# A layer norm, attention and GEGLU block on one core: one PSUM copy of the gate with the gelu on GpSimd, down tiles in pairs at a lag of five, and P times V every second step

## The chip, the cores and the metric

The kernel runs on one core of one Trainium2 chip. A core has TensorE (PE, matmuls into PSUM), VectorE (DVE), ScalarE (ACT), GpSimd (POOL) and SyncE (SP), whose queue issues nearly all DMAs here. Each engine works through its own queue in order; a wait for another engine holds everything behind it. The metric is the device time of one execution in microseconds (us), lower is better.

## The reference

```python
def _A_ref(x, wqkv, wo):                      # 32 heads of 18
    qkv = (x @ wqkv).reshape(B, S, 3, H, Dh)...
    scores = einsum("bhqd,bhkd->bhqk", q, k) * (Dh ** -0.5)
    p = softmax(scores)
    return einsum("bhqk,bhkd->bhqd", p, v)... @ wo

def _B_ref(x, w_gate, w_up, w_down):
    g = x @ w_gate
    u = x @ w_up
    return (gelu(g, approximate=True) * u) @ w_down

xn = layernorm(x)                             # (1, 2048, 576)
out = x + _A_ref(xn, ...) * silu(_B_ref(xn, ...))
```

S is 2048, the model width D 576, the hidden width F 4608. All is float32. The gelu is the tanh form: 0.5 g (1 + tanh(0.798 (g + 0.0447 g^3))).

## The kernel before

Float32 products are made from float16 pieces: the normed input is kept transposed as a high and a low part (XHT, XL), weights are split into whi and wlo, and three matmuls (high by high, high by low, low by high) are accumulated in PSUM. P times V alone runs in float32.

**Attention is the outer loop.** Heads are taken two at a time, 16 pairs, each in 32 steps (s): 2 halves of the queries (qh) by 16 blocks of 128 keys (kt). In a step qk2 makes two score tiles of 128 keys by 512 queries for two heads (L935, two matmuls of 64 rows side by side), and an exp on ScalarE writes them as P (L941). Beside each, qk1 (L895) makes a score tile of the next pair, of which DVE takes the row maxima (L898, into PM); both score tiles have one PSUM buffer each. pv (L957) multiplies P and V of the step before, four matmuls in four column strips. After step 29 max_end reduces the maxima of the next pair (L907 to L910), transposes them on PE (L916) and writes them through DRAM (md, L920) into two rows of the next pair's QT (L922). norm divides by the softmax sums, through small DMAs.

**Everything else is filler.** A generator yields the other matmuls one by one: the V and Q, K projections, then 18 chunks (c) of 256 hidden columns, each for four blocks (sb) of 512 tokens. For a chunk and block, gu makes two gate tiles g and two up tiles u (ft 0 and 1; 14 matmuls of 512 columns each, L289 to L294), and dn four down tiles of 128 tokens in two halves of 288 columns (six matmuls each, L485), which DVE accumulates into Y (L496). fill(amt) issues filler until the planned PE time amt is used up; a step calls it four times.

**Deferred work.** What follows a tile on DVE, ScalarE or GpSimd isn't issued where the tile ends but at a later tick: subtick() ahead of each fill advances a counter, issues what is due, and one piece of the next chunk's weight preparation (prep: maxima, splits L231 and L234). defer.at(now + n, f) puts f at the n-th tick from now. As each engine's queue is in order, the tick decides behind which exp or which row maximum such work stands.

**The m banks.** Gate, up and down tiles, the transpose of L916 and the projections share three PSUM banks, m, in rotation: a tile's first matmul waits until the readers of the tile three before it are done (MTile, with the number of readers).

The gelu of before reads g from PSUM three times: a square on ScalarE (L425), a product on DVE (L429), tanh on ScalarE (L434), a product with g again on DVE (L437), then with u (L450); ScalarE writes the high half of h (L459) and GpSimd the low half (L463). dn of the block before runs behind each up tile, four m tiles in a row.

Of the kernel before, what the change touches and what calls it, by code (L numbers as in the profile page):

```python
# [20 lines left out]
P = 128  # L21
NT = S // P
# [45 lines left out]
def kernel(ctx: ExitStack, tc: tile.TileContext, x, wqkv, wo, w_gate, w_up, w_down, out):  # L68
# [55 lines left out]
    def prep(name, parts, n, down=None, urgent=False, lead=0):  # L124
# [74 lines left out]
        def scales():  # L199
# [120 lines left out]
    def proj_j_sb(w, j, part, sb, mt=None, wait=0):  # L320
# [7 lines left out]
        def hi():  # L328
            ev["h"] = wp.tile([P, 512], F16, tag="evh", name=f"evh_{j}_{part}_{sb}")
            nc.scalar.activation(ev["h"][0:n], mt.t[0:n], AF.Copy, scale=2.0 ** -22)  # L330
            mt.done()

        def lo():
            ev["l"] = wp.tile([P, 512], F16, tag="evl", name=f"evl_{j}_{part}_{sb}")
# [82 lines left out]
    def gu(w, c, sb, ft):  # L417
        s0 = 512 * sb
        g = MTile([P, 512], F32, 3)
        yield from mm_wx(g.t, w, 0, P * ft, P * ft + P, s0, s0 + 512)  # L420
        st = {}

        def sq():
            st["z"] = wp.tile([P, 512], F32, tag="sz", name=f"sz_{c}_{sb}_{ft}")
            nc.scalar.activation(st["z"], g.t, AF.Square, scale=w.uE[:, 0:1])  # L425
            g.done()

        def zz():
            nc.vector.scalar_tensor_tensor(st["z"], st["z"], 1.0 / GC, g.t, op0=ALU.add, op1=ALU.mult)  # L429
            g.done()  # L430

        def th():
            st["t"] = wp.tile([P, 512], F32, tag="tw", name=f"tw_{c}_{sb}_{ft}")
            nc.scalar.activation(st["t"], st["z"], AF.Tanh, scale=w.uE[:, 1:2])  # L434

        def ww():
            nc.vector.scalar_tensor_tensor(st["t"], st["t"], 1.0, g.t, op0=ALU.add, op1=ALU.mult)  # L437
            g.done()
# [8 lines left out]
        yield from mm_wx(u.t, w, 1, P * ft, P * ft + P, s0, s0 + 512)  # L447

        def hp():
            nc.vector.scalar_tensor_tensor(st["t"], st["t"], 2.0 ** -54, u.t, op0=ALU.mult, op1=ALU.mult)  # L450
            u.done()

        def hhi():
# [5 lines left out]
            nc.scalar.activation(hstate[c, sb].hi[:, ft], st["t"], AF.Copy)  # L459

        def hlo():
            hs = hstate[c, sb]
            nc.gpsimd.tensor_tensor(hs.lo[:, ft], st["t"], hs.hi[:, ft], op=ALU.subtract)  # L463
# [9 lines left out]
    def dn(w, c, sb, tiles):  # L473
        until(lambda: (c, sb) in hstate and hstate[c, sb].n == 2)
        hs = hstate[c, sb]
        for si in tiles:
# [658 lines left out]
```

## Time and profile before

| | |
|---|---|
| median of three runs (lowest, highest) | 3055.71 us (3055.68, 3059.48) |
| the profiled execution | 3058.35 us, of which its span is 3056.6 us |
| granted TensorE clock, mean | 0.977 |
| PE busy in 1000 to 1200 us / ScalarE / DVE / GpSimd | 192.6 / 114.8 / 152.9 / 12.8 us of 200 |
| from the start to the first exp of attention | about 188 us |
| from pair to pair of heads, pairs 1 to 15 | 174.9 us |

How to read the rows of the prediction: a row of the timeline has start and length in us, then engine, line, operation, output <- inputs, shapes, and in brackets how long the engine stood idle before and what ended that. A row of waits has the engine and line that waited, what it waited for, the sum in us, how often, and the longest. A row of groups has count, then busy us and the mean ns of one, then the idle time before and its releasers. PE's records overlap, since matmuls are pipelined: starts are compared, not lengths.

### The profile page before, as it was taken

The page shows a single profiled execution, that of the slowest core. Times are in us where ns is not written, and L with a number is a line of the kernel's source. Part 1 is how long each engine was busy: PE and PEld are TensorE (multiplying, and loading weights), DVE is VectorE, ACT ScalarE, POOL GpSimd, SP SyncE. Part 2 cuts the span into 40 slices and gives each one's busy share as a digit, 9 for nine tenths or more (in the row PEclk, how much of TensorE's full clock was granted, in tenths as well). Part 3 has the DMA queues.
Part 4 walks back from the last instruction along what each step waited for, and adds up shares of the span by engine and source line. Part 5 has one row for each costly group of instructions (what it writes and reads, how often), then busy time and mean ns, then how long its engine had stood idle before and what let it go on. Part 6 is the DMA issues. An engine that isn't in the chain of part 4 may idle for free.

```text
span 3056.6 us, 43746 instructions
## 1 busy us (share of the span) xinstructions
PE 2817.5 (92%) x17732; PEld 1051.1 (34%) x17732; DVE 2229.5 (73%) x3055; ACT 1614.9 (53%) x1948; POOL 203.4 (7%) x220
## 2 busy tenths in 40 slices
PE   5899889999999999999999999999999999999877
PEld 5443223333333333333333333333333333333334
DVE  6766567777677877777786877777777868777594
ACT  4135455555565555555555555565555555565531
POOL 3000000000000000000000000000000000000000
PEclk9899999999999999999999999999999999999988
DMA  3233311010011011010101011001111010101113
GB/s 119 80 85 81 92 37 45 13 44 12 28 23 31 20 36 45 13 31 20 31 21 35 20 36 44 13 11 40 31 20 36 20 36 23 31 5 33 29 48 116
DMA packets 135872, 117.39 MB, mean 38 GB/s; under 512 B 59957, under 2 KB 113973, under 8 KB 135669
## 3 DMA queue, kind: packets, MB, share of 16 engines
q1 hardware_dynamic: 135092, 113.42, 13.5%
q8 instruction: 138, 2.26, 0.3%
q10 hardware_dynamic: 576, 1.18, 0.1%
q14 instruction: 66, 0.53, 0.1%
HBM read 84.95 MB, written 29.61 MB: 37 GB/s over the span
## 4 chain that ended last, share of the span: by engine, by line
PE 73%; DVE 18%; DMA 4%; issue 2%; ACT 2%; SPq 1%; POOL 0%; ACTq 0%; DVEq 0%; POOLq 0%
PE m L289 26%; PE pv L957 14%; PE m L485 10%; PE s L935 9%; DVE PM L898 8%; PE s L895 7%; PE m L302 2%; PE m L292 2%; PE m L294 2%; DVE sg L542 1%; DMA KD<-evh 1%; DVE tw L450 1%; DVE y L496 1%; DVE tw L437 1%; DVE m_c L163 1%
## 5 line engine op out<-in xcount | busy, mean ns | idle before, releaser
L898 DVE TENSOR_REDUCE PM<-s 128x2 f32<-128x1024 f32 x1024 | 1251.6, 1224 | 632.2 <-PE s L895 623.6
L941 ACT ACTIVATE P<-s,etab 128x1024 f32<-128x1024 f32 x896 | 997.1, 1113 | 939.1 <-PE s L935 927.5
L957 PE MATMUL pv<-P,VT 128*32 128x512 f32 x4096 | 553.1, 612 | 2.1 <-DMA VT<-VS 2.1
L289 PE MATMUL m<-XHT,whi_c 128*128 128x512 f16 x1152 | 438.5, 381 | 20.7 <-DVE y L496 18.7
L289 PE MATMUL m<-XHT,wlo_c 128*128 128x512 f16 x1152 | 439.0, 381 | 0.0
L289 PE MATMUL m<-XL,whi_c 128*128 128x512 f16 x1152 | 438.7, 381 | 0.0
L935 PE MATMUL s<-QT,KT 56*128 56x512 f16 x2048 | 403.1, 390 | 33.7 <-ACT P L941 33.2
L895 PE MATMUL s<-KT,QT 54*128 54x512 f16 x2048 | 395.8, 382 | 28.8 <-DMA QT<-QD 18.1
L485 PE MATMUL m<-dhi_c,hhi 128*128 128x288 f16 x1152 | 332.5, 289 | 62.9 <-DVE tw L450 28.8
L289 PEld LDWEIGHTS <-whi_c 128*128 128x128 f16 x2304 | 211.6, 98 | 407.8 <-issue 236.2
L463 POOL TENSOR_TENSOR hlo<-tw,hhi 128x512 f16<-128x512 f32 x144 | 167.2, 1161 | 2557.2 <-ACT hhi L459 2367.0
L485 PE MATMUL m<-dhi_c,hlo 128*128 128x288 f16 x1152 | 332.7, 289 | 0.0
L485 PE MATMUL m<-dlo_c,hhi 128*128 128x288 f16 x1152 | 332.5, 289 | 0.0
L485 PEld LDWEIGHTS <-hhi 128*128 128x128 f16 x2304 | 216.4, 98 | 271.0 <-issue 205.9
L496 DVE SCALAR_TENSOR_TENSOR y<-m,c_c,y 128x288 f32<-128x288 f32 x544 | 262.7, 504 | 13.1 <-PE m L485 12.7
L935 PEld LDWEIGHTS <-KT 56*128 56x128 f16 x2048 | 99.6, 92 | 426.1 <-issue 425.9
L289 PEld LDWEIGHTS <-wlo_c 128*128 128x128 f16 x1152 | 112.5, 98 | 205.3 <-issue 111.5
L957 PEld LDWEIGHTS pv<-P,VT 128*32 128x32 f32 x4096 | 81.2, 108 | 212.5 <-issue 209.9
L943 ACT ACTIVATE P<-s,etab 128x512 f32<-128x512 f32 x128 | 87.9, 687 | 116.2 <-PE s L935 110.5
L485 PEld LDWEIGHTS <-hlo 128*128 128x128 f16 x1152 | 112.9, 98 | 88.1 <-issue 64.0
L434 ACT ACTIVATE tw<-sz,uE_c 128x512 f32<-128x512 f32 x144 | 103.3, 717 | 58.0 <-DVE sz L429 58.0
L459 ACT ACTIVATE hhi<-tw 128x512 f16<-128x512 f32 x144 | 90.0, 625 | 66.9 <-DVE tw L450 66.9
(163 smaller groups left out, 2464.3 us busy)
## 6 DMA issues: line engine op xcount, KB each, us to landing
draw_c<-in_B_w_down SPq DMA_DIRECT2D x18, 576.0 KB
raw_c<-in_B_w_gate SPq DMA_DIRECT2D x18, 512.0 KB
raw_c<-in_B_w_up SPq DMA_DIRECT2D x18, 512.0 KB
obr<-rd SPq DMA_DIRECT2D x30, 256.0 KB
KT<-KD SPq DMA_DIRECT2D x32, 224.0 KB
QT<-QD SPq DMA_DIRECT2D x32, 216.0 KB
VS<-vst SPq DMA_DIRECT2D x16, 304.0 KB
VT<-VS SPq DMA_DIRECT2D x16, 304.0 KB
```

What stands on the lines that cost most here:

```text
L289: nc.tensor.matmul(o, lw[:, t, i, c0:c1], xx[:, t, s0:s1], start=(k == 0), stop=False)
L434: nc.scalar.activation(st["t"], st["z"], AF.Tanh, scale=w.uE[:, 1:2])
L459: nc.scalar.activation(hstate[c, sb].hi[:, ft], st["t"], AF.Copy)
L463: nc.gpsimd.tensor_tensor(hs.lo[:, ft], st["t"], hs.hi[:, ft], op=ALU.subtract)
L485: nc.tensor.matmul(mt.t[:, 0:288], a[:, ft, sl], b[:, ft, ms], start=(k == 0), stop=(k == 5))
L496: nc.vector.scalar_tensor_tensor(yy, mt.t[:, 0:288], w.c, yy, op0=ALU.mult, op1=ALU.add)
L895: nc.tensor.matmul(s1[:, h], QT[p][r, P * qt:P * qt + P], KT[p][r, 512 * kb:512 * kb + 512], start=True, stop=True)
L898: nc.vector.tensor_reduce(PM[p][:, :, qt, kb:kb + 1], s1, op=ALU.max, axis=AX.X)
L935: nc.tensor.matmul(s2[:, h], KT[p][r, P * kt:P * kt + P], QT[p][r, 512 * qb:512 * qb + 512], start=True, stop=True)
L941: nc.scalar.activation(pt, s2, AF.Exp, scale=ETAB[j0])
L943: nc.scalar.activation(pt[:, 0], s2[:, 0], AF.Exp, scale=ETAB[j0])
L957: nc.tensor.matmul(o[qd:qd + 32, :], VT[p][:, c0:c0 + 32], pt[:, h], start=(kt == 0), stop=(kt == NT - 1), skip_group_check=True,)
```

## The change

1. The gate is read from PSUM once: ScalarE copies it, scaled, to SBUF (gs). The cubic (three operations), the added one and the product with the up tile's part run on GpSimd, tanh stays on ScalarE. DVE makes u times g from PSUM and the copy (gv). The gate's m tile has one reader instead of three. The ticks of the chain change with it.
2. Down tiles are queued (dnq). Behind each gate tile and behind each up tile one 128-token unit (two m tiles) is taken, if more than five units are queued.
3. P times V is issued in every even step for the two steps before; the two fills behind it get nothing, and the other six of two steps each a third of a step's share instead of a quarter. P has six buffers instead of four.
4. max_end's transpose comes at the third tick instead of the second. The evacuation tiles evh and evl of the projections have three buffers instead of two.

```diff
@@ def prep
-                nc.vector.tensor_scalar(
-                    w.uE[:, 1:2], w.E[:, 0:1], GK * GC * 2.0 ** -24, None, op0=ALU.mult
-                )
+                nc.vector.tensor_scalar(w.uE[:, 1:2], w.s[:, 0:1], 2.0 ** -44, None, op0=ALU.mult)
@@ def proj_j_sb
-            ev["h"] = wp.tile([P, 512], F16, tag="evh", name=f"evh_{j}_{part}_{sb}")
+            ev["h"] = wp.tile([P, 512], F16, tag="evh", name=f"evh_{j}_{part}_{sb}", bufs=3)
...
@@ def gu
-        g = MTile([P, 512], F32, 3)
+        st = {}
+        gp = nc.gpsimd
+        g = MTile([P, 512], F32, 1)
         yield from mm_wx(g.t, w, 0, P * ft, P * ft + P, s0, s0 + 512)
-        def sq():
-            nc.scalar.activation(st["z"], g.t, AF.Square, scale=w.uE[:, 0:1])
-        def zz():
-            nc.vector.scalar_tensor_tensor(st["z"], st["z"], 1.0 / GC, g.t, op0=ALU.add, op1=ALU.mult)
-        def th():
-            nc.scalar.activation(st["t"], st["z"], AF.Tanh, scale=w.uE[:, 1:2])
-        def ww():
-            nc.vector.scalar_tensor_tensor(st["t"], st["t"], 1.0, g.t, op0=ALU.add, op1=ALU.mult)
+        def copy():
+            nc.scalar.activation(st["g"], g.t, AF.Copy, scale=w.uE[:, 0:1])
+            g.done()
+        def cubic():
+            gp.tensor_tensor(st["t"], st["g"], st["g"], op=ALU.mult)
+            gp.tensor_scalar(st["t"], st["t"], GC, 1.0, op0=ALU.mult, op1=ALU.add)
+            gp.tensor_tensor(st["t"], st["t"], st["g"], op=ALU.mult)
+        def th():
+            nc.scalar.activation(st["t"], st["t"], AF.Tanh, scale=GK)
+        def one():
+            gp.tensor_scalar(st["t"], st["t"], 1.0, 1.0, op0=ALU.mult, op1=ALU.add)
         t0 = defer.now
-        defer.at(t0 + 1, sq)
-        defer.at(t0 + 2, zz)
-        defer.at(t0 + 3, th)
-        defer.at(t0 + 4, ww)
+        defer.at(t0 + 1, copy)
+        defer.at(t0 + 2, cubic)
+        defer.at(t0 + 5, th)
+        defer.at(t0 + 6, one)
+        yield from dn_unit()
         u = MTile([P, 512], F32, 1)
         yield from mm_wx(u.t, w, 1, P * ft, P * ft + P, s0, s0 + 512)
+        def mul():
+            nc.vector.scalar_tensor_tensor(
+                st["v"], u.t, w.uE[:, 1:2], st["g"], op0=ALU.mult, op1=ALU.mult
+            )
+            u.done()
         def hp():
-            nc.vector.scalar_tensor_tensor(st["t"], st["t"], 2.0 ** -54, u.t, op0=ALU.mult, op1=ALU.mult)
-            u.done()
+            gp.tensor_tensor(st["v"], st["v"], st["t"], op=ALU.mult)
...
-        t1 = max(defer.now, t0 + 4)
-        defer.at(t1 + 1, hp)
-        defer.at(t1 + 2, hhi)
-        defer.at(t1 + 3, hlo)
+        t1 = defer.now
+        t2 = max(t1 + 2, t0 + 7)
+        defer.at(t1 + 1, mul)
+        defer.at(t2, hp)
+        defer.at(t2 + 2, hhi)
+        defer.at(t2 + 3, hlo)
+        yield from dn_unit()
...
+    def dn_unit(lag=5):
+        if len(dnq) > lag:
+            yield from dnq.popleft()
@@ def unit_c
         for sb in range(NB):
-            pu = prev_u[0]
-            yield from gu(w, c, sb, 0)
-            if pu is not None:
-                yield from dn(*pu, (0, 1))
-            yield from gu(w, c, sb, 1)
-            if pu is not None:
-                yield from dn(*pu, (2, 3))
+            dnq.extend(dn(w, c, sb, si) for si in range(4))
+            for ft in range(2):
+                yield from gu(w, c, sb, ft)
...
@@ def max_end
-        defer.at(defer.now + 2, b)
+        defer.at(defer.now + 3, b)
@@ def qk2
-        pt = ap.tile([P, 2, 512], F32, tag="P", name=f"P_{p}_{qb}_{kt}", bufs=4)
+        pt = ap.tile([P, 2, 512], F32, tag="P", name=f"P_{p}_{qb}_{kt}", bufs=6)
@@ the loop over steps
-                amt = left[0] / (4.0 * (2 * NT * (NPAIR - 1 - p) - s + LATE))
+                amt = left[0] / (3.0 * (2 * NT * (NPAIR - 1 - p) - s + LATE))
...
             pb = qk2(p, 2 * qh + 1, kt)
             if kp < NPAIR:
                 qk1(kp, next(items))
-            if pend is not None:
-                pv(*pend)
-            pend = (p, qh, kt, pa, pb)
-            subtick()
-            fill(amt)
-            subtick()
-            fill(amt)
+            pend.append((p, qh, kt, pa, pb))
+            if s % 2 == 0:
+                for u in pend[:-1]:
+                    pv(*u)
+                pend = pend[-1:]
+                fills(2, 0.0)
+            else:
+                fills(2, amt)
```

The order of the instructions at three places follows, with the numbers that the program gives its tiles (s2_6_1_10: scores of pair 6, query block 1, key block 10; m388: the 389th m tile); "..." stands for rows left out, the weight loads among them.

First, PE in steps 10 and 11 of pair 6. Before:

```order
L935 MATMUL s2_6_1_10_11981<-QT6_9596,KT6_9597 128x512
L895 MATMUL s1_7_25_11986<-KT7_11155,QT7_11154 128x512
L957 MATMUL pv_6_0_11523<-P_6_0_9_11920,VT6_11444 32x512 x2
L957 MATMUL pv_6_0_11523<-P_6_1_9_11939,VT6_11444 32x512 x2
L289 MATMUL m388_11958<-XHT_81,wlo_c6_10560 128x512
...
L294 MATMUL m388_11958<-XHT_81,wlo_c6_10560 128x512
L935 MATMUL s2_6_0_11_12003<-QT6_9596,KT6_9597 128x512
```

And now:

```order
L943 MATMUL s2_6_1_10_12195<-QT6_9746,KT6_9747 128x512
L903 MATMUL s1_7_25_12200<-KT7_11345,QT7_11344 128x512
L965 MATMUL pv_6_0_11790<-P_6_0_8_12075,VT6_11640 32x512 x2
L965 MATMUL pv_6_0_11790<-P_6_1_8_12105,VT6_11640 32x512 x2
L965 MATMUL pv_6_0_11790<-P_6_0_9_12127,VT6_11640 32x512 x2
L965 MATMUL pv_6_0_11790<-P_6_1_9_12148,VT6_11640 32x512 x2
L943 MATMUL s2_6_0_11_12214<-QT6_9746,KT6_9747 128x512
L903 MATMUL s1_7_26_12219<-KT7_11345,QT7_11344 128x512
L287 MATMUL m388_12173<-XHT_81,wlo_c6_10718 128x512
```

P times V of two key blocks (8 and 9) now stands in one run, and the next scores follow it with no filler between; in step 11 there is none.

Second, PE and DVE around an up tile (m400 in both) and the tile three later, which takes its bank. Before, on PE and then on DVE, m403 is a down tile:

```order
L294 MATMUL m400_12245<-XHT_81,wlo_c6_10560 128x512
L485 MATMUL m401_12294<-dhi_c6_10684,hhi_6_2_11876 128x288
...
L895 MATMUL s1_7_39_12303<-KT7_11155,QT7_11154 128x512
L485 MATMUL m402_12316<-dhi_c6_10684,hhi_6_2_11876 128x288
L485 MATMUL m403_12330<-dhi_c6_10684,hhi_6_2_11876 128x288
L898 TENSOR_REDUCE PM7_11160<-s1_7_39_12303 128x2
L450 SCALAR_TENSOR_TENSOR tw_6_3_1_12286<-tw_6_3_1_12286,m400_12245 128x512
L982 RECIPROCAL oc_6_0_12268<-oc_6_0_12268 128x16
L496 SCALAR_TENSOR_TENSOR y_3674<-m401_12294,c_c6_10533,y_3674 128x288
```

Now m401 and m402 are the two halves of one down unit and m403 is the next gate:

```order
L292 MATMUL m400_12462<-XHT_81,wlo_c6_10718 128x512
L495 MATMUL m401_12516<-dhi_c6_10839,hhi_6_2_12120 128x288
L943 MATMUL s2_6_3_1_12518<-QT6_9746,KT6_9747 128x512
L903 MATMUL s1_7_39_12523<-KT7_11345,QT7_11344 128x512
L495 MATMUL m401_12516<-dlo_c6_10840,hhi_6_2_12120 128x288
...
L495 MATMUL m402_12534<-dhi_c6_10839,hlo_6_2_12121 128x288
L287 MATMUL m403_12548<-XHT_81,whi_c7_11964 128x512
L906 TENSOR_REDUCE PM7_11350<-s1_7_39_12523 128x2
L451 SCALAR_TENSOR_TENSOR gv_6_3_1_12527<-m400_12462,uE_c6_10692,gs_6_3_1_12454 128x512
L990 RECIPROCAL oc_6_0_12495<-oc_6_0_12495 128x16
```

The instruction that frees m400 stands on DVE behind the row maxima of the same scores in both; the tile that waits for it is a gate instead of a down tile, and behind the scores come no P times V but eleven down matmuls, five of m401 and six of m402.

Third, the chain of one gate tile (chunk 7, block 3, ft 0) on ScalarE and on GpSimd. Before, on ScalarE, and the one row of GpSimd:

```order
L425 ACTIVATE sz_7_3_0_13374<-m442_13334,uE_c7_11794 128x512
L941 ACTIVATE P_7_0_7_13382<-s2_7_0_7_13379,etab2_2369 128x1024
L434 ACTIVATE tw_7_3_0_13392<-sz_7_3_0_13374,uE_c7_11794 128x512
L941 ACTIVATE P_7_1_7_13401<-s2_7_1_7_13398,etab2_2369 128x1024
L941 ACTIVATE P_7_0_8_13424<-s2_7_0_8_13421,etab2_2369 128x1024
L459 ACTIVATE hhi_7_3_13438<-tw_7_3_0_13392 128x512
L463 TENSOR_TENSOR hlo_7_3_13439<-tw_7_3_0_13392,hhi_7_3_13438 128x512
```

Now, on ScalarE and then on GpSimd:

```order
L424 ACTIVATE gs_7_3_0_13594<-m440_13552,uE_c7_11936 128x512
L949 ACTIVATE P_7_1_6_13608<-s2_7_1_6_13605,etab2_2365 128x1024
L949 ACTIVATE P_7_0_7_13631<-s2_7_0_7_13628,etab2_2365 128x1024
L434 ACTIVATE tw_7_3_0_13622<-tw_7_3_0_13622 128x512
...
L465 ACTIVATE hhi_7_3_13713<-gv_7_3_0_13680 128x512
L429 TENSOR_TENSOR tw_7_3_0_13622<-gs_7_3_0_13594 128x512
L430 TENSOR_SCALAR tw_7_3_0_13622<-tw_7_3_0_13622 128x512
L431 TENSOR_TENSOR tw_7_3_0_13622<-tw_7_3_0_13622,gs_7_3_0_13594 128x512
L437 TENSOR_SCALAR tw_7_3_0_13622<-tw_7_3_0_13622 128x512
L457 TENSOR_TENSOR gv_7_3_0_13680<-gv_7_3_0_13680,tw_7_3_0_13622 128x512
L469 TENSOR_TENSOR hlo_7_3_13714<-gv_7_3_0_13680,hhi_7_3_13713 128x512
```

Between the copy and tanh stand two exps instead of one, and tanh waits for three operations of GpSimd instead of one of DVE.

More of the change, by code (lines that the diff above doesn't have):

```diff
@@ L333, in lo @@
         def lo():
-            ev["l"] = wp.tile([P, 512], F16, tag="evl", name=f"evl_{j}_{part}_{sb}")
+            ev["l"] = wp.tile([P, 512], F16, tag="evl", name=f"evl_{j}_{part}_{sb}", bufs=3)
             nc.vector.scalar_tensor_tensor(
@@ L560, in zero_last @@
     def zero_last():
-        z = wp.tile([P, 512], F16, tag="evh", name="zeros")
+        z = wp.tile([P, 512], F16, tag="evh", name="zeros", bufs=3)
         nc.gpsimd.memset(z, 0.0)
@@ L1048, with fills @@
     zero_last()
-    pend = None
+    pend = []
+    def fills(n, amt):
+        for _ in range(n):
+            subtick()
+            fill(amt)
     for p in range(NPAIR):
@@ L1092 @@
         pass
-    pv(*pend)
+    for u in pend:
+        pv(*u)
     while not last_o.get(1):
```

91 lines of the change are left out of this document (42 added, 49 removed).

## The prediction

> **What bounds the kernel now.** The page comes first: shares of the engines, then the chain.
>
> ```profile
> PE 2817.5 (92%) x17732; PEld 1051.1 (34%) x17732; DVE 2229.5 (73%) x3055; ACT 1614.9 (53%) x1948; POOL 203.4 (7%) x220
> PE 73%; DVE 18%; DMA 4%; issue 2%; ACT 2%; SPq 1%; POOL 0%; ACTq 0%; DVEq 0%; POOLq 0%
> ```
>
> TensorE carries the span, DVE is second, GpSimd is nearly idle. A busy PE is not yet a PE at its peak, so the timeline of one step is read next (start, length, instruction).
>
> ```profile
> 1001.02 0.39 PE L935 MATMUL s<-QT,KT 56*128 56x512 f16 x2
> 1002.43 0.38 PE L289 MATMUL m<-XHT,whi_c 128*128 128x512 f16 x1
> 1002.65 0.38 PE L289 MATMUL m<-XL,whi_c 128*128 128x512 f16 x1
> 1002.96 0.39 PE L935 MATMUL s<-QT,KT 56*128 56x512 f16 x2
> 1003.19 0.38 PE L895 MATMUL s<-KT,QT 54*128 54x512 f16 x2
> 1003.45 1.11 ACT L941 ACTIVATE P<-s,etab 128x1024 f32<-128x1024 f32 x1 [0.83 <-PE s L935]
> 1003.50 1.06 PE L957 MATMUL pv<-P,VT 128*32 128x512 f32 x8
> 1003.61 1.23 DVE L898 TENSOR_REDUCE PM<-s 128x2 f32<-128x1024 f32 x1 [0.71 <-PE s L895]
> 1004.50 0.39 PE L289 MATMUL m<-XHT,wlo_c 128*128 128x512 f16 x1
> 1006.11 0.39 PE L935 MATMUL s<-QT,KT 56*128 56x512 f16 x2
> ```
>
> Two 512-column matmuls of one kind start 0.22 us apart (1002.43, 1002.65), though each record is 0.38 long. Where the kind changes (128-row filler, 64-row scores, 32-column P times V) the step is 0.31: filler to scores 1002.65 to 1002.96, scores to PV 1003.19 to 1003.50. **A change of kind costs 0.31 - 0.215 = 0.095 us**, and no row of waits names it. A step has two score pairs and lasts 5.1 us here (1001.02 to 1006.11), a half step 2.55. The waits view gives what PE does wait for (us in total, times, longest):
>
> ```profile
> PE m L485 <- DVE tw L450: 28.8, 40, 1.5
> PE m L916 <- DVE rmc L910: 25.2, 15, 1.9
> PE m L485 <- DVE y L496: 23.7, 35, 1.3
> PE m L289 <- DVE y L496: 18.7, 29, 1.3
> PE m L485 <- DVE tw L437: 8.8, 12, 1.0
> PE s L935 <- ACT P L941: 33.2, 12, 10.7
> ACT evh L330 <- DMA KD<-evh: 18.1, 5, 6.2
> ```
>
> Four rows are waits for one of the three m banks: 28.8 + 23.7 + 18.7 + 8.8 = 80 us in 116 waits. A record outlasts the spacing by about 0.17 (next fence: 0.29 long, 0.12 apart), which hides that much of each: 80 + 116 x 0.17 = **100 us**. So PE loses about 100 us to m banks, 28 to one transpose per pair (25.2 + 15 x 0.17), and, at five changes of kind in each of 512 steps, 243 to those.
>
> How an m wait comes about:
>
> ```profile
> 1043.50 0.38 PE L895 MATMUL s<-KT,QT 54*128 54x512 f16 x2
> 1043.92 1.23 DVE L898 TENSOR_REDUCE PM<-s 128x2 f32<-128x1024 f32 x1 [0.66 <-PE s L895]
> 1044.56 0.29 PE L485 MATMUL m<-dlo_c,hhi 128*128 128x288 f16 x1
> 1044.68 0.29 PE L485 MATMUL m<-dhi_c,hlo 128*128 128x288 f16 x1
> 1045.07 0.68 DVE L450 SCALAR_TENSOR_TENSOR tw<-tw,m 128x512 f32<-128x512 f32 x1
> 1045.80 0.28 PE L485 MATMUL m<-dhi_c,hhi 128*128 128x288 f16 x1 [0.83 <-DVE tw L450]
> ```
>
> The instruction that frees the bank (L450) stands on DVE behind the 1.23 us reduction of the scores just made; PE has run out of down matmuls by 1044.80 and stands 1.0 us. Everything behind it on PE, the next scores above all, waits too.
>
> **The change, part by part.** The sum starts from the profiled execution, 3058.35 us (span 3056.6); the median of the runs is 3055.71, so 2.6 us lower, and I forecast on the former.
>
> *P times V by two steps.* The listing keeps every matmul. Two steps had ten changes of kind (four filler to scores, two scores to filler, two scores to PV, two PV to filler); now eight (three, three, one, and one PV to scores). PV to scores is in no row: its cost lies between nothing and two changes, 0.19. At 0.095, the nearest rows, 512 steps save 512 x 0.095 = **48.6**; the ends are 73 (nothing) and 24 (0.19). What covers the emptied ticks: PV of two units lasts about 1.8 us, so the score pairs stay some 2.5 us apart. Six P tiles hold the three units that are live at once, so no exp waits for one: nothing.
>
> *The m banks.* A gate's bank is now freed by one ScalarE copy, an up bank by one DVE product, and four down tiles in a row, which waited for each other's accumulation, become two and two. Down tiles therefore no longer wait: a gate or up tile of 3 us stands ahead of the second use of each of their banks, and their inputs, made five tiles ahead, are long there. But the gate now takes the bank of the up tile 12 short matmuls (1.46 us) ahead, and the up tile that of the gate, 12 ahead. In the listing shown, the up tile ends ahead of a scores pair; on DVE its product stands behind that pair's reduction. From the start of L895's pair: reduction after 0.42 for 1.23, product 0.68 (L450's form), signal 0.05, so free at 2.38; PE gets there at 0.31 + 11 x 0.122 = 1.65. PE stands 0.73. Counted so over the listing, 72 of 144 gates come 0.9 us too early on average (64 us) and 83 of 144 up tiles 0.63 (52 us; the copy stands behind an exp): 116 us. The same count over the old listing gives 135, where the waits show 100, so it runs a third high: 116 x 100 / 135 = 86. Between -14 (86) and +16 (116) I take **0**: the wait moves from the down tiles to the gate and up tiles. The ends are -100 (none left) and +30.
>
> *The transpose of the maxima* comes one tick later, behind PV, and its 27.7 us go: DVE's L910 is long done there. It puts the two DMAs behind it closer to the next pair's first scores, now two half steps (5.1 us) later. The rows for the first pair:
>
> ```profile
> 181.48 0.32 PE L916 MATMUL m<-ident,rmc 128*64 128x128 f16 x1
> 182.87 0.51 SPq L920 DMA_DIRECT2D md<-rms  x1
> 188.10 0.39 PE L935 MATMUL s<-QT,KT 56*128 56x512 f16 x2
> ```
>
> From the first issue to the scores were 5.2 us at most, plus some 0.5 ahead of it where DVE is free. So between nothing and 0.6 us at 15 pairs, more where SP is held by other DMAs: **+2** (0 to 20).
>
> *A third evh and evl buffer* takes off ScalarE waits of 18.1 us in the projections; what of them reaches PE is part of the 33.2 (whose longest, 10.7, is another chain): **-5** (0 to -18). The last 150 us, where DVE's reciprocals of the output gate set the end, keep their order on DVE: nothing.
>
> *The chain on GpSimd.* Six operations for each of 144 tiles instead of one, and two fewer on DVE. The rows nearest:
>
> ```profile
> L463 POOL TENSOR_TENSOR hlo<-tw,hhi 128x512 f16<-128x512 f32 x144 | 167.2, 1161 | 2557.2 <-ACT hhi L459 2367.0
> L677 POOL TENSOR_TENSOR ft<-ft,ob 128x576 f32<-128x576 f32 x4 | 5.9, 1471 | 149.6 <-DVE ob L643 130.1 <-DVE ft L672 19.5
> L425 ACT ACTIVATE sz<-m,uE_c 128x512 f32<-128x512 f32 x144 | 98.2, 682 | 10.4 <-PE m L294 10.4
> L434 ACT ACTIVATE tw<-sz,uE_c 128x512 f32<-128x512 f32 x144 | 103.3, 717 | 58.0 <-DVE sz L429 58.0
> ```
>
> At 1.16 to 1.31 us (1471 x 512/576) this is 144 x 6 x 1.2 = 1040 us of GpSimd, 40% of the stretch, so no bound. The one-input forms have no row; I take 1.2 too (bounds 0.68, ScalarE's L425, and 1.5). What can hurt is order: tanh stands in ScalarE's queue two exps behind the copy (124 of 144 tiles; 20 have four), and behind it the exp for which PE's scores bank waits. Copy to tanh is at least a half step and an exp, 2.55 + 1.11 = 3.7 us; three operations take 3.5 to 3.9. So ScalarE waits 0.2 at times, and has 0.9 to spare in each half step (2.55 less 1.11 and 0.5 of other work: 1614.9 / 1024 half steps, less 1.11): **+3** (0 to 40).
>
> A second way to be hurt stands in the prologue, where GpSimd was busy:
>
> ```profile
> 66.88 1.38 POOL L781 TENSOR_TENSOR xn<-xt,xn 128x512 f16<-128x512 f32 x1
> 67.16 1.70 DVE L234 SCALAR_TENSOR_TENSOR wlo_v<-raw_v,s_v,whi_v 128x576 f16<-128x576 f32 x1
> 72.53 1.53 DVE L234 SCALAR_TENSOR_TENSOR wlo_v<-raw_v,s_v,whi_v 128x576 f16<-128x576 f32 x2
> ```
>
> One split took 1.70 us beside a GpSimd operation, the last two 0.77 each with none: 0.9 for a meeting. Some 220 DVE instructions read two SBUF tiles (the splits L234 and L245, norm's L989 and L1003); with GpSimd busy 40% some 90 meet one, 79 us of DVE. DVE gets 196 back (144 x 2 x 0.68), and a reduction may be 0.9 late before PE's next scores want its bank, so little of it shows: **+5** (0 to 79). The Trainium skill (SBUF — State Buffer, "Who interferes with whom") has the rule: a DVE instruction with two SBUF inputs and a GpSimd instruction that reads SBUF lock each other out for its whole length. The 0.9 agrees. By it the reductions and the products, with at most one SBUF tile, stay untouched, and the sum stands.
>
> Sum: 3058.35 - 48.6 + 0 - 27.7 + 2 - 5 + 3 + 5 = **2987**.
>
> **The rivals.**
>
> *The m waits vanish.* If the release is usually ahead of PE (the reduction starts earlier, ticks fall luckily), the 100 us go: 2887. For it: DVE sheds work. Against: the product stands behind the same 1.23 us reduction.
>
> *Doubled ticks.* Behind PV two ticks now come without filler between, so two batches of deferred work land on ScalarE at once: an exp, a copy (L425's form) and a tanh, 1.11 + 0.68 + 0.72 = 2.5, against 2.5 between scores. If each of 256 such places costs 0.25 us, 64 us are given back: 3051. Against: one gate in some 3.5 steps, so seldom both.
>
> *GpSimd and DVE in each other's way.* If DVE has no slack where they meet (the split ahead of a product that frees a bank), all 79 us are PE's: 3061; half of it, 3024. Against: 90 meetings are spread over 1024 half steps, and PE waits for DVE in some 72 of them.
>
> *GpSimd too slow: slower than before.* If an operation takes over (3.7 + 0.9) / 3 = 1.53 us, tanh holds ScalarE, the exp comes late and PE stands at L935 in every tile; the gain of 71 us (0.5 a tile) is gone from 1.7 us. At 2.0 it is 144 x (6.0 - 4.6) = 202: 3189. Against: the rows shown are 1.16 to 1.38, the longest beside a DVE split.
>
> **How the numbers follow.** Forecast 0.55 (own range 2935 to 3030), vanished waits 0.15, doubled ticks 0.11, each other's way 0.10, slow GpSimd 0.09. The range runs from inside the vanished waits to the doubled ticks, 2895 to 3050, leaving about 0.08 below and 0.12 above. A measurement tells 0.2% (6 us) from no change. Faster: 0.55 + 0.15 + half of the doubled ticks and most of each other's way, 0.84; same 0.06; slower 0.10.
>
> **What would show it.** Right: changes of kind fewer by a fifth at the same 0.31, the scores about 1.9 us behind the start of a double PV (2 x 0.9 + 0.095); no row L485 for tw; new rows of waits of PE at the gate and up matmuls for the DVE product and the ScalarE copy, 60 to 120 us together; no wait at the transpose; GpSimd about 1040 us busy, tanh waiting for it under 0.4 each. Wrong: GpSimd operations over 1.5 us, PE waiting at the scores for exps, or no waits at gate and up.

## The result and the profile after

The changed kernel takes **2990.32 us** (median; 2987.10 to 2992.59), the kernel before, beside it, 3057.60; the ratio is 0.9777, interval 0.976 to 0.9794. The forecast was 2987, range 2895 to 3050. Timed a second time it took 2990.17. So the sum held to 3 us. Whether its terms did is another matter, and most of what follows is about that.

The engines' shares in the page after, busy us, share of the span and instructions:

```profile
PE 2747.0 (92%) x17732; PEld 1099.0 (37%) x17732; DVE 2107.9 (71%) x2767; ACT 1595.3 (53%) x1948; POOL 916.6 (31%) x940
```

And from the view of waits after, PE's (what it waited for: us in total, times, longest):

```profile
PE m L287 <- DVE gv L451: 60.3, 72, 4.0
PE m L287 <- ACT gs L424: 40.7, 61, 2.7
PE s L903 <- DVE PM L906: 21.4, 31, 3.7
PE s L943 <- ACT P L949: 12.2, 10, 5.0
PE m L287 <- DVE y L506: 4.0, 5, 1.4
PE s L943 <- DMA QT<-md: 2.1, 1, 2.1
```

PE has lost 70 us of busy time with the same number of matmuls, DVE 122, and GpSimd has taken on 713. In the waits the rows for the old L485 are gone: down tiles don't wait. In their place gate and up tiles (both L287) wait for the product and for the copy, 105.0 us in 138 waits with the row for y, where before it was 80 in 116. The product's row has the 72 waits that were counted in the listing ahead of the run. The transpose waits for nothing, and its DMA, moved later, holds PE once, for 2.1 us. The timeline around one up tile after, on PE and DVE (rows between these are left out):

```profile
1003.44 0.38 PE L292 MATMUL m<-XHT,wlo_c 128*128 128x512 f16 x1
1004.71 0.38 PE L903 MATMUL s<-KT,QT 54*128 54x512 f16 x2
1005.13 1.23 DVE L906 TENSOR_REDUCE PM<-s 128x2 f32<-128x1024 f32 x1 [1.24 <-PE s L903]
1005.65 0.29 PE L495 MATMUL m<-dhi_c,hlo 128*128 128x288 f16 x1
1006.27 0.74 DVE L451 SCALAR_TENSOR_TENSOR gv<-m,uE_c,gs 128x512 f32<-128x512 f32 x1
1007.07 0.38 PE L287 MATMUL m<-XHT,whi_c 128*128 128x512 f16 x1 [1.14 <-DVE gv L451]
1008.78 1.92 PE L965 MATMUL pv<-P,VT 128*32 128x512 f32 x16
1010.63 0.39 PE L943 MATMUL s<-QT,KT 56*128 56x512 f16 x2
```

The up tile ends at 1003.66 (the start of L292 and one spacing). DVE is idle for 1.24 us until 1005.13; the product could run in that time, but it is issued at the next tick, so it stands behind the row maxima of scores that came later, and ends at 1007.01. PE has had no down matmul to issue since 1005.77 and stands 1.3 us. The last two rows show the double PV: 1.85 us from its start to the next scores, where one PV took 1.00 before (1003.50 to 1004.50): two of 1.00 have become 1.85, 0.15 less, of which 0.095 is the change of kind behind the first PV. With the one ahead of the second, 0.095 again, two steps save 0.24 us, and 256 of them 60.

The groups of GpSimd after (count, then busy us, mean ns, idle before):

```profile
L457 POOL TENSOR_TENSOR gv<-gv,tw 128x512 f32<-128x512 f32 x144 | 187.5, 1302 | 396.8 <-DVE gv L451 363.9 <-DVE oc L990 17.5 <-PE s L903 5.7
L429 POOL TENSOR_TENSOR tw<-gs 128x512 f32<-128x512 f32 x144 | 153.6, 1066 | 697.7 <-ACT gs L424 697.7
L430 POOL TENSOR_SCALAR tw<-tw 128x512 f32<-128x512 f32 x144 | 96.0, 667 | 12.6
L437 POOL TENSOR_SCALAR tw<-tw 128x512 f32<-128x512 f32 x144 | 90.2, 626 | 299.7 <-ACT tw L434 299.7
```

The two-input forms are as expected (1.07 to 1.30 us), the one-input forms half of the 1.2 that was taken, so GpSimd is busy 917 us, not 1040.

### The profile page after: what moved, and what is told of

The parts are those of the page before. It is cut to its first block, busy times and chain, and to the rows that moved or that the text cites. A ratio compares the mean times of both kernels' runs of the same rounds, so it can differ in the third digit from the quotient of the medians.

```text
span 2988.0 us, 44281 instructions
## 1 busy us (share of the span) xinstructions
PE 2747.0 (92%) x17732; PEld 1099.0 (37%) x17732; DVE 2107.9 (71%) x2767; ACT 1595.3 (53%) x1948; POOL 916.6 (31%) x940
## 3 DMA queue, kind: packets, MB, share of 16 engines
q8 instruction: 138, 2.26, 0.3%
## 4 chain that ended last, share of the span: by engine, by line
PE 71%; DVE 14%; DMA 6%; ACT 5%; issue 3%; SPq 1%; POOL 0%; ACTq 0%; DVEq 0%; POOLq 0%
PE m L287 26%; PE pv L965 14%; PE s L943 10%; PE m L495 8%; PE s L903 7%; DVE PM L906 4%; PE m L300 2%; PE m L290 2%; PE m L292 2%; DVE gv L451 2%; ACT P L949 2%; ACT gs L424 1%; DMA obr<-rd 1%; DVE sg L550 1%; DMA sd<-osb 1%
## 5 line engine op out<-in xcount | busy, mean ns | idle before, releaser
L906 DVE TENSOR_REDUCE PM<-s 128x2 f32<-128x1024 f32 x1024 | 1251.8, 1224 | 730.8 <-PE s L903 726.2
L287 PE MATMUL m<-XHT,whi_c 128*128 128x512 f16 x1152 | 440.4, 382 | 105.7 <-DVE gv L451 60.3
L965 PE MATMUL pv<-P,VT 128*32 128x512 f32 x4096 | 495.0, 601 | 0.0
L287 PE MATMUL m<-XHT,wlo_c 128*128 128x512 f16 x1152 | 441.1, 383 | 7.5 <-DVE wlo_c L232 7.5
L287 PE MATMUL m<-XL,whi_c 128*128 128x512 f16 x1152 | 441.5, 383 | 0.0
L903 PE MATMUL s<-KT,QT 54*128 54x512 f16 x2048 | 394.7, 380 | 41.2 <-DVE PM L906 21.4
L943 PE MATMUL s<-QT,KT 56*128 56x512 f16 x2048 | 401.9, 388 | 14.4 <-ACT P L949 12.2
L429 POOL TENSOR_TENSOR tw<-gs 128x512 f32<-128x512 f32 x144 | 153.6, 1066 | 697.7 <-ACT gs L424 697.7
L287 PEld LDWEIGHTS <-whi_c 128*128 128x128 f16 x2304 | 216.7, 98 | 384.9 <-issue 220.3
L457 POOL TENSOR_TENSOR gv<-gv,tw 128x512 f32<-128x512 f32 x144 | 187.5, 1302 | 396.8 <-DVE gv L451 363.9
L469 POOL TENSOR_TENSOR hlo<-gv,hhi 128x512 f16<-128x512 f32 x144 | 167.9, 1166 | 355.1 <-ACT hhi L465 355.1
L965 PEld LDWEIGHTS pv<-P,VT 128*32 128x32 f32 x4096 | 107.1, 109 | 255.9 <-issue 255.9
L431 POOL TENSOR_TENSOR tw<-tw,gs 128x512 f32<-128x512 f32 x144 | 186.1, 1293 | 12.0
L437 POOL TENSOR_SCALAR tw<-tw 128x512 f32<-128x512 f32 x144 | 90.2, 626 | 299.7 <-ACT tw L434 299.7
L287 PEld LDWEIGHTS <-wlo_c 128*128 128x128 f16 x1152 | 112.9, 98 | 170.4 <-issue 58.3
```

The lines of the kernel that those rows point to most:

```text
L287: nc.tensor.matmul(o, lw[:, t, i, c0:c1], xx[:, t, s0:s1], start=(k == 0), stop=False)
L429: gp.tensor_tensor(st["t"], st["g"], st["g"], op=ALU.mult)
L431: gp.tensor_tensor(st["t"], st["t"], st["g"], op=ALU.mult)
L457: gp.tensor_tensor(st["v"], st["v"], st["t"], op=ALU.mult)
L469: gp.tensor_tensor(hs.lo[:, ft], st["v"], hs.hi[:, ft], op=ALU.subtract)
L903: nc.tensor.matmul(s1[:, h], QT[p][r, P * qt:P * qt + P], KT[p][r, 512 * kb:512 * kb + 512], start=True, stop=True)
```

## The experiments

All times are medians. Runs of different rounds are compared to some 3 us: the kernel before, timed beside each round, took 3054.7 to 3057.9. "m waits" are PE's waits for one of the three m banks, as the rows have them and in how many waits. A record hides some 0.17 us of each (the prediction shows how), so 105.0 in 138 stands for 128.

### One part alone

*P times V by two steps, on the kernel before.*

```diff
-            if pend is not None:
-                pv(*pend)
+            if s % 2 == 0:
+                for u in pend[:-1]:
+                    pv(*u)
+                pend = pend[-1:]
+                fills(2, 0.0)
+            else:
+                fills(2, amt)
```

> The kernel before with P times V by two steps alone (six P buffers, the emptied fills); gelu, down tiles, transpose and evacuation as before. Theory (PV by two steps carries the gain): the profile of the changed kernel shows a single PV run of 1.00 us to the next kind and a double one of 1.86, so two steps save two changes of kind and about 0.04 us, 256 x 0.235 = 60 us; 3058 - 60 = about 2998 us (2985 to 3012). Rival 1 (doubled ticks take it back, up to 64 us, without the new chain): 3030 to 3065. Rival 2 (the gain belongs to the gelu chain and the order of the down tiles): above 3035 here, and the next run below 3020.

Measured: **3084.27 us**, ratio 1.0096 (1.0081 to 1.0111). The part that was to carry the gain makes the old kernel slower by 30 us. Rival 2's two conditions hold (above 3035 here, the next run below 3020), but none of the three expectations had a kernel slower than before. Its waits of PE:

```profile
PE m L485 <- DVE tw L437: 47.2, 39, 1.9
PE m L485 <- DVE tw L450: 41.1, 51, 1.9
PE m L289 <- DVE y L496: 36.9, 45, 1.8
PE m L485 <- DVE y L496: 35.8, 46, 1.9
```

161.0 us in 181 waits instead of 80 in 116: with the hidden part 192 instead of 100. The changes of kind that go (60 us) are paid for by 92 us of m waits.

*The gelu chain and the down units, without PV by two, third tick and third buffers* (of the edit, the lines for buffers and for the share of each fill are left out):

```diff
-            if s % 2 == 0:
-                for u in pend[:-1]:
-                    pv(*u)
-                pend = pend[-1:]
-                fills(2, 0.0)
-            else:
-                fills(2, amt)
+            if pend is not None:
+                pv(*pend)
...
-        defer.at(defer.now + 3, b)
+        defer.at(defer.now + 2, b)
```

> The changed kernel with P times V in every step, the transpose at the second tick and two evh and evl buffers, as before: the gelu chain on GpSimd and the two-tile down units stand alone. Theory (they only move the m waits from the down tiles to gate and up tiles): the waits of PE at gate and up matmuls for the product and the copy are some 100 us in 130 waits as in the changed kernel, against 80 in 116 before, so 3056 + 0 to 30 us: 3050 to 3090 us. Rival (this part carries the gain): 3020 or less.

Measured: **3009.07 us**, ratio 0.9842 (0.9828 to 0.9857). The rival's number: this part brings 46 us. The rows that are left:

```profile
PE m L287 <- DVE gv L451: 26.2, 32, 1.1
PE m L287 <- ACT gs L424: 17.6, 32, 1.0
PE m L924 <- DVE rmc L918: 16.8, 14, 1.3
```

43.8 us in 64 m waits, with the hidden part 55 where it was 100.

*The same with four down tiles in a row* behind each up tile (two units there, none behind the gate):

```diff
         defer.at(t0 + 6, one)
-        yield from dn_unit()
...
         defer.at(t2 + 3, hlo)
         yield from dn_unit()
+        yield from dn_unit()
```

> The kernel with the chain alone (3009 us; P times V in every step, second tick), with two down units (four m tiles) behind each up tile and none behind the gate, as before the change. Tells which part of the chain's change halved the m waits (100 us before, 57 with the chain). Theory A (the order two and two): down tiles wait for one another's accumulation again, rows of PE at L495 for L506 of 20 us and more, m waits 85 to 110, time 3030 to 3060. Theory B (the bank of the gate has one early reader instead of three): m waits stay below 65 and time within 12 us of 3009.

Measured: **3035.00 us**, ratio 0.9930 (0.9911 to 0.9949). Theory A by the time; down tiles wait for y again, 18.2 us in 28, and the m waits are 64.6 in 90 (80 with the hidden part), a little under A's range. So the order two and two is worth 26 of the chain's 46 us. The other 20 belong to the new chain; how much of them is its one early reader of the gate, and how much the work that DVE sheds, no run parts.

### What frees the bank

*Copy and product issued right behind the last matmul of their tile*, on the changed kernel:

```diff
-    def mm_wx(o, w, i, c0, c1, s0, s1):
+    def mm_wx(o, w, i, c0, c1, s0, s1, end=None):
...
         nc.tensor.matmul(o, w.lo[:, 4, i, c0:c1], XT[:, s0:s1], start=False, stop=True)
+        if end is not None:
+            end()
         yield 0.216
...
-        yield from mm_wx(g.t, w, 0, P * ft, P * ft + P, s0, s0 + 512)
+        yield from mm_wx(g.t, w, 0, P * ft, P * ft + P, s0, s0 + 512, copy)
-        defer.at(t0 + 1, copy)
...
+        until(lambda: "g" in st)
...
-        yield from mm_wx(u.t, w, 1, P * ft, P * ft + P, s0, s0 + 512)
+        yield from mm_wx(u.t, w, 1, P * ft, P * ft + P, s0, s0 + 512, mul)
-        defer.at(t1 + 1, mul)
```

The line with until goes through ticks until the copy has been issued, so that the product finds it; here it always has been.

> The changed kernel with the ScalarE copy and the DVE product issued right after the last matmul of their gate or up tile, instead of at the next tick. Theory (a gate or up tile waits because the instruction that frees its bank stands behind an exp or a row maximum of scores that were made after the tile): the two rows of PE at L287 (60 us in 72 for the product, 41 in 61 for the copy; with 0.17 hidden in each, 124 us) fall below 45 us together, and the time falls by 60 to 110 us: 2880 to 2930. Rival 1 (the engines are simply busy then, in whatever order): waits stay above 80 us, time within 15 us of 2990. Rival 2 (ScalarE and DVE now stand waiting for the tile's end and make the next exp and row maximum late): m waits fall, waits at the scores rise by as much, 2970 to 3010.

Measured: **2890.89 us**, ratio 0.9458 (0.9443 to 0.9474). The theory, at the lower half of its range, and faster than both kernels: 99 us below the changed one with the same instructions. Its rows:

```profile
PE s L904 <- DVE PM L907: 33.3, 43, 3.7
PE s L944 <- ACT P L950: 15.6, 17, 5.0
PE m L287 <- DVE gv L451: 6.3, 13, 0.9
PE m L287 <- ACT gs L424: 0.4, 1, 0.4
```

The two rows went from 101 to 6.7 us. Row maxima and exps come a little later for it (33.3 and 15.6, from 21.4 and 12.2), rival 2 in small. A tile's product on DVE in its timeline:

```profile
1029.73 0.75 DVE L451 SCALAR_TENSOR_TENSOR gv<-m,uE_c,gs 128x512 f32<-128x512 f32 x1 [0.70 <-PE m L292]
1030.39 1.22 DVE L907 TENSOR_REDUCE PM<-s 128x2 f32<-128x1024 f32 x1
```

Now DVE stands idle for the tile's end (0.70, released by L292), and the reduction comes behind the product.

*The product alone* right behind its tile (the edit above without the copy's lines; the line with until stays):

> The changed kernel with the DVE product alone right behind its up tile; the copy stays at the next tick. Theory (each release is late on its own): the row of PE at L287 for the product goes (60 us in 72, 73 with the hidden part), that for the copy stays at 35 to 50; time 2990 - 60 to 75: 2915 to 2930. Rival (gate and up waits feed one another: a gate that no longer waits brings PE early to the up tile): the copy's row grows by 20 us or more and the time is 2940 to 2970.

Measured: **2940.18 us**, ratio 0.9622 (0.9606 to 0.9638). The rows are the theory's (product 6.9 us in 13, copy 45.2 in 62), the time is 10 us above its range: 50 us are won. With the hidden part the product's row fell by 63, but other rows grew by 10: the copy's from 40.7 to 45.2, that for row maxima from 21.4 to 25.5, that for y from 4.0 to 5.4. So the one wait feeds the others a little, and a wait's price with the hidden part is an upper bound. So product and copy share the gain evenly, 50 and 49.

### What PV by two is worth

*The kernel with early copy and product, with P times V in every step:*

```diff
-                amt = left[0] / (3.0 * (2 * NT * (NPAIR - 1 - p) - s + LATE))
+                amt = left[0] / (4.0 * (2 * NT * (NPAIR - 1 - p) - s + LATE))
...
-            if s % 2 == 0:
-                for u in pend[:-1]:
-                    pv(*u)
-                pend = pend[-1:]
-                fills(2, 0.0)
-            else:
-                fills(2, amt)
+            for u in pend[:-1]:
+                pv(*u)
+            pend = pend[-1:]
+            fills(2, amt)
```

> The kernel with copy and product right behind their tile (2891 us), with P times V in every step and filler in all fills. Theory (with the m waits out of the way, PV by two is worth its changes of kind, 256 x 0.235 = 60 us): 2940 to 2960 us. Rival (PV by two is worth nothing on this chain, as 3008 with it and 3009 without it at the second tick say): 2885 to 2905.

Measured: **2939.04 us**, ratio 0.9609 (0.9595 to 0.9623), a hair under the theory's range: where no m wait stands behind it, PV by two is worth 48 us (46 by the two ratios).

*The same edit on the changed kernel*, where copy and product come by ticks:

> The changed kernel with P times V in every step and filler in all fills; chain, third tick and third evh buffer stay. It prices PV by two inside the change as made. Theory (with copy and product at the next tick, PV by two costs more in m waits than it saves in changes of kind: 57 us with the chain alone, 128 with PV by two, against 48 to 60 saved): m waits near 57 us again, and the time is some 16 us below the changed kernel: 2965 to 2982 us, faster without this part. Rival (the two cancel): 2985 to 2998. Rival of the prediction (PV by two is worth 48.6): 3025 to 3045.

Measured: **2987.13 us**, ratio 0.9768 (0.9754 to 0.9781). That is the rival's number and the changed kernel's time within the intervals: **inside the change as it was made, PV by two is worth nothing.** The rows say where its gain went: with PV in every step the waits for product and copy are

```profile
PE m L287 <- DVE gv L451: 26.2, 32, 1.1
PE m L287 <- ACT gs L424: 18.2, 31, 1.8
```

44.4 us in 63, 55 with the hidden part, against 105.0 and 128 with PV by two: 61 to 73 us more, which takes back the 60 of the changes of kind. That the two then cancel rather than leave a loss goes with scores that wait less for exps (27.5 us in this kernel, 12.2 with PV by two) and P times V that no longer waits for its V (6.7, none). Against these, filler waits more for DVE: 7.5 us for the split wlo_c, none before, and 21.3 for ob at the end, 14.0 before. My theory had none of this; it missed the time by 5 us.

*Filler behind the double PV as well*, all eight fills of two steps alike:

```diff
-                amt = left[0] / (3.0 * (2 * NT * (NPAIR - 1 - p) - s + LATE))
+                amt = left[0] / (4.0 * (2 * NT * (NPAIR - 1 - p) - s + LATE))
...
-                fills(2, 0.0)
+                fills(2, amt)
```

> The changed kernel with all eight fills of two steps filled alike (a quarter of a step's share each), so filler also stands behind the double PV. It has nine changes of kind in two steps, not eight: by that alone 256 x 0.095 = 24 us slower than the changed kernel. Theory (PV by two made the m waits, since six fills carry what eight carried: a third more filler between two ticks, and what frees a bank comes by ticks): the rows of PE at L287 for the product and the copy fall from 101 us in 133 towards the 44 us in 64 that the kernel with the chain alone has, so -50 + 24: 2955 to 2975 us. Rival (the m waits come from the double PV itself, which holds scores and row maxima together): they stay above 85 us and the time rises to 3005 to 3025.

Measured: **3020.13 us**, ratio 0.9879 (0.9865 to 0.9894). My theory, that a third more filler between ticks makes the waits, fell: they stay at 92.7 us in 128, and the time is the rival's. So most of them come with the double PV itself, and the timelines show how. For each of 143 up tiles I took the time from its end (the start of its last matmul and one spacing of 0.216) to PE's arrival at the next gate, and to the end of the product that frees the bank:

| kernel | PV lies between | PE arrives, without / with PV between | the product ends |
|---|---|---|---|
| changed kernel | 31% | 1.97 / 4.60 us | 2.66 us |
| the same with PV in every step | 59% | 2.00 / 3.53 us | 2.48 us |
| early copy and product | 31% | 1.97 / 4.71 us | 1.48 us |

(Means, worked out from starts and ends in the timelines; gate tiles give much the same, with the copy's end at 2.50, 2.26 and 1.07.) P times V of a single step, standing between an up tile and the next gate, was **the cover under which the bank came free**: PE arrives at 3.5 us with it, at 2.0 without. It also covered the right tiles: it stands behind the scores whose reduction makes the product late, and with PV in every step the product ends at 2.74 in the tiles with PV between, at 2.12 in the others. Put two by two, it covers half as many tiles, with more than they need. In the changed kernel 68 of the 73 such waits over 0.06 us have no PV in between; with PV in every step it is 30 of 51. Issued early, the release ends at 1.48 on average, ahead of PE either way.

### The small parts

*The transpose at the second tick again*, on the changed kernel (`defer.now + 2`).

> The changed kernel with the transpose of the maxima at the second tick again. Theory (the transpose waited for the reduction of the maxima, which is late by about 1.8 us a pair at that place): the row of PE at the transpose for L918 returns with about 25 us in 15, and the time rises by 22 to 30 us: 3012 to 3021. Rival (what the transpose lost was covered by other waits): 2985 to 3000.

Measured: **3007.82 us**, ratio 0.9843 (0.9829 to 0.9858): 17.5 us (20 by the ratios), under the theory's range, above the rival's. The waits are back, 20.4 us in 13 for the reductions and 3.2 in 2 for a product, but the row for the product falls from 60.3 to 49.4 at the same time. I read it so that DVE catches up while PE stands at the transpose; no run shows that by itself.

*The changed kernel once more, and with two evh and evl buffers again:*

> The changed kernel once more, unchanged, as the neighbour of the next two runs on the same chip: 2985 to 2996 us.

> The changed kernel with two evh and evl buffers again. Theory of the prediction (a third buffer takes 5 us off, 0 to 18): ScalarE's row for evh waiting for KD goes from 2.1 us back to some 15 to 18, and the time is 3 to 18 us above the changed kernel beside it. Rival (PE doesn't feel it): within 3 us of it. That PE's waits at the scores for exps went from 33 to 12 us may be this or the order; if it is this, that row comes back to 30 us.

Measured: 2990.17 us, ratio 0.9779 (0.9764 to 0.9793), and with two buffers **3007.76 us**, ratio 0.9839 (0.9824 to 0.9853): 17.6 us, the top of the prediction's bounds. ScalarE's row for evh behind KD goes from 2.3 to 16.4, PE's row at the scores for exps from 12.2 to 22.9. The timeline with two buffers (PE) shows what else:

```profile
357.85 0.61 PE L943 MATMUL s<-QT,KT 56*128 56x512 f16 x2 [7.71 <-ACT P L949]
358.23 0.66 PE L903 MATMUL s<-KT,QT 54*128 54x512 f16 x2
358.82 0.64 PE L287 MATMUL m<-XHT,whi_j 128*72 128x512 f16 x1
359.25 0.63 PE L287 MATMUL m<-XL,whi_j 128*72 128x512 f16 x1
359.68 0.63 PE L287 MATMUL m<-XHT,wlo_j 128*72 128x512 f16 x1
...
363.87 0.38 PE L287 MATMUL m<-XHT,wlo_j 128*72 128x512 f16 x1
364.09 0.38 PE L287 MATMUL m<-XHT,whi_j 128*72 128x512 f16 x1
```

PE stands 7.71 us for an exp that stands behind evh, and then its matmuls start 0.43 us apart for some 5 us, not 0.22.

*More work on GpSimd*, behind hlo in the changed kernel:

```diff
             gp.tensor_tensor(hs.lo[:, ft], st["v"], hs.hi[:, ft], op=ALU.subtract)
+            for _ in range(3):
+                gp.tensor_tensor(st["t"], st["g"], st["g"], op=ALU.mult)
```

> The changed kernel with three more GpSimd products of two SBUF tiles behind each hlo (into the tw tile, which nothing reads then; the output is the same): 432 x 1.07 = 460 us more GpSimd work, 1380 of 2988. Theory (GpSimd's work beside DVE's reaches PE hardly: DVE's splits lost 24 us by it in the changed kernel): DVE's two-input instructions get longer once more, some 10 to 15 us of DVE, time 2985 to 3005. Rival 1 (they are in each other's way, and DVE's delay is PE's): 3010 to 3040. Rival 2 (GpSimd's queue gets late: tanh, h): waits of ScalarE for GpSimd above 50 us, above 3020.

Measured: **3018.34 us**, ratio 0.9865 (0.9848 to 0.9881): 28 us for 463 us of GpSimd. ScalarE now waits for GpSimd ahead of tanh, its row of waits:

```profile
ACT tw L434 <- POOL tw L431: 43.2, 38, 3.8
```

The split on DVE that reads two SBUF tiles, in the view of groups of the same kernel, takes 1190 ns, against 992 in the changed kernel and 810 before:

```profile
L243 DVE SCALAR_TENSOR_TENSOR dlo_c<-draw_c,s_c,dhi_c 128x576 f16<-128x576 f32 x36 | 42.1, 1190 | 0.0
```

The time is in the first rival's range, the sign of the second (43.2 us, in the changed kernel 1.4) is there too: it asked for more than 50 us and 3020. PE's rows show some of both. Its waits for row maxima grow from 21.4 to 30.7, all of the growth behind DVE instructions that took longer than usual; those for exps grow from 12.2 to 19.7 and those for copies from 40.7 to 46.0, both ScalarE's. That is 22 of the 28 us. The run does say that GpSimd had little room left in its order: half as much work again takes back 28 of the 67 us.

## Why the prediction was right

**Right as a sum, with several terms that the runs price otherwise.** Point by point:

- *P times V by two steps, -48.6.* The mechanism is right and well sized: eight changes of kind instead of ten at 0.095 (the traces have 2701 changes among scores, PV and filler before, 2171 now), a double PV of 1.85 us where 1.9 was forecast, 60 us in all, and 48 us on the clock where nothing hides it. But the ends of 73 and 24 don't hold the worth of this part: alone it costs 30 us, in the change it is worth nothing. The step that failed is "What covers the emptied ticks": it asked whether the scores keep their distance, and not what the moved PV itself had been covering, the release of m banks.
- *The m banks, 0.* It was **28 us** (from 100 to 128 with the hidden part, 25 by the rows alone), at the edge of the bounds given. The count over the listing was good: 64 us in 72 gates counted, 60.3 in 72 measured (72 with the hidden part); 52 in 83 up tiles counted, 40.7 in 61 measured (51). The step that failed is scaling it by 100/135: the old listing's error didn't carry over. And this 0 is two large parts in one: the chain and the order two and two take 45 us away, PV by two adds 73. Because the count was made over the whole changed listing it held both, and so the sum came out; had the parts been asked for one by one, the forecast would have had their order of worth wrong.
- *The transpose, -27.7.* The wait is gone as forecast; its worth is 17.5. With the stall the product's row is 11 us shorter: waits of PE don't add up one to one.
- *The DMA of md, +2.* One wait of 2.1 us.
- *evh, -5.* Under-sized: 17.6. The row of PE's waits (the "33.2" with other chains in it) was read for the stall alone; of the 17.6 some 10.7 stand in that row, some 2 are the half-speed stretch behind the stall (ten starts 0.21 us late), which no term had, and the rest the runs don't place.
- *tanh, +3.* ScalarE waits 1.4 us in 4, since the one-input forms take 0.63 to 0.67 us: the term was too high by nearly all of it.
- *DVE and GpSimd, +5.* The mechanism is right, and it was worth some **11 us**. The splits and onl got longer by 24 us of DVE (wlo_c 787 to 852 ns, dlo 810 to 992, onl 682 to 1039), a third of the 79 that bounded it, while osb, with two SBUF tiles too, stays at 686. PE feels it where the prediction looked, at scores that wait for late row maxima: that row grew from 10.0 us in 12 to 21.4 in 31. In 15 of the 31 waits, 10.8 us, the reduction stands behind a DVE instruction that took at least 0.25 us more than usual; before it was one wait, 0.9 us. The longest of the 15 are behind an instruction of 128x1, the last of a chunk's scales, which the prediction didn't count (c_c, 159 ns on average before, 387 now):

```profile
572.68 1.28 POOL L431 TENSOR_TENSOR tw<-tw,gs 128x512 f32<-128x512 f32 x1
572.97 1.01 DVE L220 TENSOR_TENSOR c_c<-c_c,E_c 128x1 f32<-128x1 f32 x1
573.90 1.21 DVE L906 TENSOR_REDUCE PM<-s 128x2 f32<-128x1024 f32 x1
575.16 0.39 PE L903 MATMUL s<-KT,QT 54*128 54x512 f16 x2 [1.27 <-DVE PM L906]
```

The product of 128x1 ends with the GpSimd operation beside it, 0.85 us late, and the scores stand 1.27 us. The row maxima themselves are 1224 ns in all three traces, before, after and with more work on GpSimd. The rule cited from the Trainium skill (SBUF — State Buffer, "Who interferes with whom") has DVE instructions with at most one SBUF input untouched, outside the 2-port modes that a tensor_scalar can enter. The row maxima agree.
- *The last 150 us, nothing.* PE's waits for ob there went from 14.1 to 21.3 us. Three waits for the first chunk's wlo_c, 7.5 us near 380 us, had no term either. Both rows are there with PV by two alone (20.5 and 7.6), which has no chain on GpSimd, so they go with PV by two.

The rivals: the m waits did not vanish in this change, but 2891 us is what the kernel takes when they do, and the prediction had put 2887 there. Doubled ticks show in no row: the scores' waits for exps are fewer than before. GpSimd and DVE are in each other's way, for 11 us and not for 37 to 79. GpSimd was fast enough.

So, by the rows, the sum left out or under-priced losses of about 49 us: 28 for the m banks (with the hidden part; what the transpose brought less than forecast stands in this row), 6 for DVE and GpSimd, 7 for ob and 7.5 for wlo_c. It under-priced gains, or over-priced losses, by about 37: 11 for PV, 13 for evh, 3 for tanh, and some 10 us of waits at the scores for exps that are gone and that no term had (33.2 to 12.2, of which the third buffer is about half). By these the time would be 12 us above the forecast, where it was 3; the other 9 us no row places. The signs and the mechanisms can be read in the profile; that the sum came out within 3 us is luck.

## What to carry to other kernels

Before work on the critical engine is bundled to save changes of kind, ask what it has been covering where it stands: a piece of it between a tile's end and the next use of its buffer may be the slack that the release lives on. Then issue what frees a shared buffer right behind the work that fills it, ahead of anything that arrives later in that engine's queue; here that alone, on top of the change, was worth more (99 us) than the whole change (67). And price parts of a change in pairs: a term that is counted over the finished order holds the price of every other part in it.

## What the runs showed of the hardware

- A stall of PE of 7.7 us is followed by about 5 us at half its rate: 512-column matmuls start 0.427 us apart, then 0.216 again; the granted clock of that stretch (350 to 365 us) is 0.66, where it is 1.00 without the stall. The Trainium skill (TensorE: Matmul & The Clock Gate, "Part 1: The HAM clock gate") has it so, half the clock after an idle window of some 3.4 us until a busy one has passed, with windows that run free of the kernel. This trace agrees in the rate (426.7 ns stated), and 5 us, more than one window and less than two, fits a stall that ends inside a window.
- Within a run of P times V a further step's four matmuls take 0.86 us, a single one with the change behind it 1.00.
- On GpSimd a product of 128x512 float32 takes 1.07 us where both inputs are the same tile and 1.30 where they differ; a scale and add 0.63 to 0.67.
- Beside a GpSimd operation, small DVE instructions on SBUF can take five or six times as long and end with it: the product of 128x1 1.01 us instead of 0.16, and a tensor_scalar of 128x2 with one input (E_c, at 571.03 us) 0.89 instead of 0.17, ending at 571.92 where GpSimd's product ends at 571.89.
